# Identity products on TensorE ahead of the first input, a second queue allowed for a load, and a new order of work

## The chip, the cores and the metric

The kernel runs on one core of a Trainium2 chip. The metric is the device time of one execution in microseconds (us). The engines are named as in the profile: PE is TensorE's matrix products, PEld its loads of the stationary operand, DVE is VectorE, ACT is ScalarE, POOL is GpSimd, SP is SyncE, which here only issues DMAs.

## The reference, cut to what matters

Two sequence models run side by side on 2048 steps of 640 channels, and their outputs are put next to each other. The first is a diagonal complex state-space recurrence, the second a gated long convolution.

```python
def _A_ref(x, Lambda_re, Lambda_im, B_re, B_im, C_re, C_im, log_dt, Dskip):
    Lam = Lambda_re + 1j * Lambda_im
    dt = jnp.exp(log_dt)
    Lam_bar = jnp.exp(dt * Lam)
    B_bar = ((Lam_bar - 1.0) / Lam)[:, None] * Bmat
    Bu = jnp.einsum("bld,pd->blp", x + 0j, B_bar)
    for t in range(L):
        h = Lam_bar[None, :] * h + Bu[:, t, :]
    y = 2.0 * jnp.einsum("blp,dp->bld", hseq, Cmat).real + x * Dskip[None, None, :]

def _B_ref(q, k, v, shift_k, ssm_k, ssm_D):
    k_shift = k_shift + k_pad[:, t:t + S, :] * shift_k[:, ks - 1 - t]   # four taps
    kv = k_shift * v
    y = irfft(rfft(kv) * rfft(ssm_k))[:, :S] + kv * ssm_D
    return q * y

return jnp.concatenate([a, b], axis=-1)
```

## The kernel before

**Tiling.** The 640 channels are five blocks of 128, with index j for the states of the first model and G for the channels of the second (there called group). Time in the first model is split into four phases s of 512 steps each (steps 4m + s), so that one scan over 512 steps serves four.

**First model.** `x{s}` loads phase s of x by a DMA that transposes (line 182, on SyncE's queue, 0.66 MB each). `B{j}` loads the real and the imaginary rows of B (line 176, two DMAs each). For j = 0 and 1 TensorE transposes B by products with the identity (`bt{j}`, line 480) and the result is copied to BT (`be{j}`, line 462 on ScalarE, 460 on VectorE); for j = 2, 3, 4 it multiplies B by a diagonal of gamma instead (`bg`, lines 494 to 497), for which VectorE builds the diagonals (`dG`, line 381, tile H). `v{s}_{j}` is the group of products that makes the input of phase s for block j: five products with x for the real part and five for the imaginary part (line 515), and, for all phases but s = 1, two more each with the evicted state of the phase before and a diagonal of Lam_bar (lines 517 and 518, 14 products in all); `ve{s}_{j}` evicts it. The diagonals are `dL` (line 381, tile diagL). So a group with s = 2 needs `ve1` of its block, one with s = 3 needs `ve2`. Phase 0 is turned by a table of sines and cosines (`rs`), scanned (`sc`, line 544) and turned back (`ra`, `rout`); `oa`, `od` (lines 556 to 564) carry the states to the other phases. `p{i}_{s}` projects 128 steps of phase s to the output (20 products of 320 columns, line 577, and six for the skip, line 582), `yo` evicts it (line 599, ScalarE), `yd` stores it.

**Parameters.** A short chain on VectorE and ScalarE makes the numbers of the first model from five small loads `lv0` to `lv4`: `tv` transposes them on TensorE (line 322), `tve` copies them out, then `exp`, `rho`, `rr`, `Fi` (lines 350 to 361), the sine and cosine `trig1` (line 368, 163, 164), `lam` (lines 375 to 378), `dL`, and gamma (`den`, lines 408 to 411, and `gam`, lines 418 to 426, nine small operations, on GpSimd where the table says so). `diagD` and `drhs`, `dcol` (lines 381, 248, 256) are for the skips.

**Second model.** For each of five groups G: k and v come by transposing loads; `kS` is a copy of k with its halves exchanged (line 618 on VectorE, 616 on ScalarE); `tap` is the four-tap filter on TensorE (line 641), `kv` the product with v (line 646). The long convolution is a Fourier transform in two steps on TensorE: `s1h`, `s1k` (line 657) and `s2h`, `s2k` (line 670) for the filter and for kv, each with evictions of 1024 columns to As_h, As_kv, Hf, Xs; then the product of the two spectra on VectorE, in two halves (`ya`, `y`, lines 682 to 688); then four inverse steps (`inv`, lines 696 to 699) evicted to zz (`zs`), two transposing DMAs of zz (`zt`), two final steps on TensorE (`fin`, line 715), the product with q on VectorE (`ob`, line 720) and the store (`od_`). The halves of `y` feed two inverse steps each.

**What sets the order.** No scheduler runs. A plan names 165 or so steps with an engine, a cost and what they need, and a table of text, ORDER, gives the order in which they are issued. Each engine works its own steps strictly in that order, each waiting for what it needs. `@n` after a name is the PSUM buffer that the step uses (four buffers of two banks, 0, 2, 4, 6), `!` sends the step to its other engine. ORDER was found by a search over a model of the engines, outside the kernel.

Of the kernel before, what the change touches and what calls it, by code (L numbers as in the profile page):

```python
# [919 lines left out]


ORDER = """
lv3! pc lsk lv4! lv0 B0 pc2 dc3 dc lv2! zer lv1! pc3 dc2 B1 pk dsel x1 gp0 tsk@0 bt0@2 gp1 tske@0 dS0 tv@4 be0@2 tve@4 bt1@6 pp
x2 drhs dD exp dcm@0 be1@6 rho Fi rr den v1_0@4 tp0 dcol@0 trig1 G0 prr lam tp1 v1_1@2 dL1 x3 pow ve1_0@4 dL0 tab1 dL2 ve1_1!@2
v2_0@6 gam! tab0 kT0 G1 tp3 dG B2 v2_1@0 tp2 x0 tab3 ve2_0!@6 gp3 tab2 v3_0@4 ve2_1!@0 gp2 kS0 B4 aRM tp4 vT0 G3 dRM tap0_0@2
hp0 tap0_1@6 ve3_0!@4 tab4 bg0@0 dS1 v0_0@4 bge0!@0 H0 B3 hp1 CT0 H1 hp2 kv0_0@2 v3_1@0 ve0_0@4 kv0_1@6 hp3 H2 hs0 rs0 bg3@2
kvo0 ve3_1@0 bg1@4 kT1 sc0 H3 bg2@6 v0_1@0 bge2@6 ra0 bge3@2 bge1@4 rout0 v1_2@6 oa2_0 ve0_1@0 od2_0 G2 v1_3@2 rs1 CT1 ve1_2@6
ca0 v2_2@4 sc1 ve1_3@2 kvs0 kS1! had0 oa3_0 vT1 s1h0_3@0 s1h0_1@6 od3_0 v2_3@2 s1he0_1@6 ra1 s1he0_3@0 ve2_2@4 rout1 s1h0_0@6
oa2_1 ve2_3@2 tap1_1@0 od2_1 s1he0_0@6 s1h0_2@4 v3_2@2 s1he0_2@4 oa1_1 cs0 tap1_0@6 qi0 ve3_2@2 od1_1 hs1 s1k0_2@4 ca1 v0_2@2
dS2 kT2 kv1_0@6 s1ke0_2@4 kv1_1@0 s1k0_3@6 cs1 ve0_2@2 s2h0_0@4 s2h0_2@0 s1ke0_3@6 v3_3@2 rs2 s2he0_0@4 kvo1 s2he0_2@0 sc2  # L930
s1k0_1@6 ve3_3@2 s2h0_1@4 s1k0_0@0 s1ke0_1@6 v0_3@2 ra2 s1ke0_0@0 s2he0_1@4 rout2 oa2_2 s2k0_1@6 ve0_3@2 kS2 s2k0_0@0 vT2
s2h0_3@4 s2ke0_1@6 had1 od2_2 v1_4@2 s2ke0_0@0 rs3 s2he0_3@4 kvs1 s2k0_3@6 ve1_4@2 s2k0_2@0 s1h1_0@4 sc3 s2ke0_3@6 v2_4@2
s2ke0_2@0 s1he1_0@4 ya0_0 tap2_0@6 ve2_4@2 s1h1_3@0 kv2_0@6 tap2_1@4 s1he1_3@0 s1k1_3@2 kT3 kv2_1@4 s1k1_0@6 s1ke1_3@2 s1k1_2@0
dS3 s1ke1_0@6 s1h1_1@4 s1h1_2@2 nH s1ke1_2@0 v3_4@6 y0_0 kvo2 hs2 s1he1_1@4 ya0_1 s1he1_2@2 s2h1_0@0 ve3_4@6 s2h1_3@4 y0_1
s1k1_1@2 kS3! v0_4@6 ra3 s1ke1_1@2 rout3 vT3 s2he1_0@0 oa2_3 inv0_2@2 ve0_4@6 od2_3 inv0_1@0 zs0_2@2 tap3_0@6 had2 rs4 s2he1_3@4
s2h1_2@2 kvs2 zs0_1@0 inv0_0@4 sc4 s2he1_2@2 s2h1_1@0 zs0_0@4 inv0_3@2 s2he1_1@0 s2k1_0@4 kv3_0@6 zs0_3@2 s2k1_3@0 ra4 s2k1_2@6
s2ke1_0@4 zt0_0 tap3_1@2 s2ke1_2@6 rout4 s2k1_1@4 oa2_4 s2ke1_3@0 p1_0@6 kT4 kv3_1@2 s2ke1_1@4 od2_4 s1k2_0@0 dS4 kvo3 yo1_0@6
s1k2_1@4 zt0_1 p0_2@2 oa3_2 s1ke2_0@0 od3_2 s1ke2_1@4 oa1_0 p0_0@6 od1_0 yo0_2@2 kS4! ya1_1 yd1_0 yd0_2 s1k2_3@0 yo0_0@6 vT4
s1k2_2@4 s1h2_0@2 y1_1 s1ke2_3@0 p2_0@6 s1ke2_2@4 ya1_0 kvs3 s1he2_0@2 yd0_0 inv1_2@0 yo2_0@6 y1_0 fin0_0@4 yd2_0 zs1_2@0
s1h2_1@2 inv1_3@6 ob0_0@4 s1he2_1@2 fin0_1@0 oa1_3 zs1_3@6 s1h2_2@4 s1h2_3@2 ob0_1@0 s1he2_2@4 inv1_1@6 hs3 s1he2_3@2 od1_3  # L940
inv1_0@4 od_0 zs1_1@6 s2h2_1@0 oa3_4 s2k2_3@2 zs1_0@4 s2k2_1@6 od3_4 s2he2_1@0 zt1_1 p2_2@4 s2ke2_3@2 oa1_2 s2ke2_1@6 od1_2
s2k2_2@0 oa1_4 yo2_2@4 s2k2_0@2 s2ke2_2@0 od1_4 s2h2_0@6 tap4_0@4 s2he2_0@6 oa3_3 s1k3_1@0 s2ke2_0@2 yd2_2 s1k3_3@6 zt1_0
kv4_0@4 s1ke3_1@0 s1k3_0@2 od3_3 s1ke3_0@2 tap4_1@4 s1ke3_3@6 s1k3_2@0 s2h2_3@2 had3 ya2_0 s1ke3_2@0 s1h3_3@6 qi1 s2he2_3@2
s2h2_2@0 s2he2_2@0 kv4_1@4 fin1_1@2 s1he3_3@6 s1h3_1@0 y2_0 kvo4 s1h3_0@4 s1he3_1@0 s1h3_2@6 hs4 ya2_1 s1he3_0@4 inv2_1@0
s1he3_2@6 inv2_0@4 zs2_1@0 s2h3_0@6 y2_1 zs2_0@4 fin1_0@0 ob1_1@2 s2he3_0@6 inv2_3@4 kvs4 ob1_0@0 inv2_2@6 zs2_3@4 s2k3_0@2
zs2_2@6 oa3_1 od_1 s2k3_1@0 s2h3_1@4 s2ke3_0!@2 s2ke3_1@0 zt2_1 s2h3_3@6 s2he3_1@4 s2he3_3!@6 s2k3_3@0 s2k3_2@2 s2ke3_3@0 p0_1@4
od3_1 s2ke3_2@2 had4 ya3_0 s2h3_2@6 yo0_1@4 s1h4_1@0 s2he3_2@6 y3_0 s1h4_0@2 p1_1@4 s1he4_1@0 zt2_0 ya3_1 s1he4_0@2 s1k4_0@6
yo1_1@4 y3_1 s1h4_3@0 s1h4_2@2 s1ke4_0@6 inv3_0@4 yd0_1 s1he4_2!@2 s1he4_3@0 yd1_1 inv3_2@6 qi2 inv3_3@0 zs3_2@6 zs3_0!@4
inv3_1@2 zs3_3@0 fin2_1@6 zs3_1!@2 p0_3@4 zt3_1 s1k4_1@0 ob2_1@6 yo0_3@4 fin2_0@2 yd0_3 s1k4_2@4 s1ke4_1!@0 zt3_0 s1k4_3@6
s1ke4_2@4 ob2_0@2 s1ke4_3@6 s2h4_2@0 s2h4_3@4 s2he4_2!@0 s2k4_3@6 s2he4_3@4 s2k4_1@2 od_2 s2ke4_3@6 s2k4_2@0 p3_2@4 s2ke4_2@0  # L950
s2ke4_1@2 ya4_1 s2k4_0@6 yo3_2@4 s2h4_1@0 y4_1 s2ke4_0@6 yd3_2 s2h4_0@2 p1_2@4 s2he4_1@0 qi3 s2he4_0!@2 ya4_0 inv4_2@6 yo1_2@4
inv4_3@0 y4_0 yd1_2 zs4_2@6 fin3_1@2 zs4_3@0 fin3_0@4 inv4_1@6 ob3_1@2 inv4_0@0 zs4_1@6 ob3_0@4 p3_1@2 zs4_0@0 od_3 zt4_1 p3_3@6
zt4_0 p1_3@4 p2_1@0 qi4 yo1_3@4 yd1_3 p3_0@4 yo2_1@0 yd2_1 yo3_1@2 yd3_1 fin4_0@0 yo3_0@4 fin4_1@2 ob4_0@0 yd3_0 p2_3@4 yo3_3@6
ob4_1@2 yd3_3 od_4 yo2_3@4 yd2_3
"""


# [66 lines left out]
```

## Time and profile before

| | us |
|---|---|
| median of three runs | 204.2 |
| lowest, highest | 203.26, 204.62 |
| profiled execution, its time | 204.2 |
| profiled execution, its span | 202.3 |

| engine | busy us of the span |
|---|---|
| PE | 186.3 |
| DVE | 167.8 |
| ACT | 153.3 |
| POOL | 27.0 |

The profile is one execution, read from its first instruction to its last; 1.9 us of its time lie outside that span. A row of the timeline has the start, the duration, the engine, the source line, the operation, what it writes and reads, how many of them are merged, and in brackets how long the engine was idle before it and what ended that. Products of TensorE are pipelined: a product of 512 columns is given 0.38 us, though the next one starts sooner, so the spacing of starts says more than the duration, and a busy TensorE isn't one at its peak. A row of the grouped view has the count, the total, the mean in ns, and the idle time ahead of the group.

### The profile page before, as it was taken

How to read it: one execution, taken by the hardware profiler on the slowest of the kernel's cores; microseconds unless marked ns; L12 is line 12 of the kernel's file. 1: busy time of each engine (PE TensorE's matmuls, PEld its weight loads, DVE VectorE, ACT ScalarE, POOL GpSimd, SP SyncE). 2: the span in 40 equal slices, each digit the busy share in tenths (PEclk: the TensorE clock that was granted, in tenths of full speed). 3: DMA queues.
4: the chain of work that ended last, by engine and by line, in shares of the span. 5: the costliest groups of instructions: out<-in, count | busy, mean ns of one | idle time of the engine just before them, and what ended most of it. 6: DMA issues, size and time to landing. Idle time of an engine off the chain costs nothing.

```text
span 202.3 us, 7486 instructions
## 1 busy us (share of the span) xinstructions
PE 186.3 (92%) x3330; PEld 128.3 (63%) x3330; DVE 167.8 (83%) x277; ACT 153.3 (76%) x188; POOL 27.0 (13%) x64
## 2 busy tenths in 40 slices
...
GB/s 115 215 220 252 222 212 217 197 185 177 66 145 200 115 3 19 243 132 135 95 249 222 191 91 186 187 200 143 165 177 169 119 192 127 146 84 196 171 133 136
DMA packets 124909, 32.61 MB, mean 161 GB/s; under 512 B 120903, under 2 KB 124236, under 8 KB 124876
## 3 DMA queue, kind: packets, MB, share of 16 engines
...
q8 instruction: 26, 0.43, 0.8%
...
## 4 chain that ended last, share of the span: by engine, by line
PE 33%; DVE 16%; ACT 9%; issue 3%; DVEq 0%
PE ps L577 15%; PE ps L670 5%; ACT Hf L462 2%; PE ps L657 2%; DVE rot L563 2%; DVE vT L646 2%; ACT zz L462 2%; DVE rot L682 2%; DVE hs L564 2%; DVE Xs L683 2%; PE ps L582 2%; PE ps L715 1%; PE ps L696 1%; ACT As_h L462 1%; DVE rot L556 1%
## 5 line engine op out<-in xcount | busy, mean ns | idle before, releaser
L515 PE MATMUL ps<-xT,BT 128*128 128x512 bf16 x200 | 50.6, 393 | 2.1 <-DMA xT<-in_A_x_dram 2.1
L577 PE MATMUL ps<-Cs,hs 128*128 128x320 bf16 x240 | 36.3, 299 | 0.2
L515 PEld LDWEIGHTS <-BT 128*128 128x128 bf16 x200 | 19.3, 101 | 25.8 <-issue 5.9
L599 ACT CAST BT<-ps 128x640 bf16<-128x640 f32 x16 | 11.0, 692 | 27.4 <-PE ps L582 26.6
L577 PEld LDWEIGHTS <-hs 128*128 128x128 bf16 x240 | 22.0, 98 | 8.1
L720 DVE TENSOR_TENSOR qb<-ps,qb 128x1024 bf16<-128x1024 f32 x10 | 11.9, 1219 | 15.7 <-PE ps L715 15.4
L670 PEld LDWEIGHTS <-G 128*64 128x64 bf16 x640 | 19.4, 112 | 5.3 <-issue 4.3
L462 ACT CAST As_kv<-ps 128x1024 bf16<-128x1024 f32 x19 | 18.5, 1027 | 2.1 <-PE ps L657 2.1
L462 ACT CAST zz<-ps 128x1024 bf16<-128x1024 f32 x18 | 18.0, 1040 | 1.7 <-PE ps L699 1.7
L462 ACT CAST Xs<-ps 128x1024 bf16<-128x1024 f32 x19 | 18.6, 1059 | 0.5 <-PE ps L670 0.5
L462 ACT CAST As_h<-ps 128x1024 bf16<-128x1024 f32 x19 | 18.6, 1031 | 0.3 <-PE ps L657 0.3
L696 PE MATMUL ps<-Xs,H 128*128 128x128 bf16 x80 | 17.5, 219 | 1.0 <-ACT As_h L462 0.5
L462 ACT CAST Hf<-ps 128x1024 bf16<-128x1024 f32 x17 | 17.6, 1044 | 0.3 <-PE ps L670 0.3
L699 PE MATMUL ps<-Xs,H 128*128 128x128 bf16 x80 | 17.5, 219 | 0.0
L698 PE MATMUL ps<-Xs,H 128*128 128x128 bf16 x80 | 17.5, 219 | 0.0
L697 PE MATMUL ps<-Xs,H 128*128 128x128 bf16 x80 | 17.5, 219 | 0.0
L682 DVE TENSOR_TENSOR rot<-Xs,Hf 128x2048 bf16<-128x2048 bf16 x10 | 12.3, 1226 | 3.4 <-ACT Xs L462 2.7
L688 DVE TENSOR_TENSOR Xs<-Xs,rot 128x1024 bf16<-128x1024 bf16 x20 | 12.9, 688 | 0.3
L670 PE MATMUL ps<-As_h,G 128*64 128x128 bf16 x320 | 12.7, 227 | 0.3 <-DVE As_kv L460 0.2
L683 DVE TENSOR_TENSOR Xs<-Xs,Hf 128x2048 bf16<-128x2048 bf16 x10 | 12.2, 1225 | 0.5
L670 PE MATMUL ps<-As_kv,G 128*64 128x128 bf16 x320 | 11.2, 220 | 1.1 <-issue 0.4
L641 PE MATMUL ps<-kT,diagS 64*64 64x512 bf16 x80 | 11.0, 391 | 1.2 <-DVE vT L646 1.2
...
## 6 DMA issues: line engine op xcount, KB each, us to landing
...
```

Source lines behind the costliest of these rows:

```text
L462: self.nc.scalar.copy(out=out, in_=in_)
L515: mm(o, lhsT=self.BT[:, r, k, j * 128:(j + 1) * 128], rhs=xT[:, k, :], start=(k == 0), stop=(s == 1 and k == NT - 1))
L577: mm(o[:, 0:320], lhsT=h[:, r, ts], rhs=self.Cs[:, r, j, c0:c0 + 320], start=(j == 0 and r == 0), stop=(not on_pe and j == NT - 1 and r == 1))
L670: self.nc.tensor.matmul(o[64 * e:64 * e + 64, c:c + 128], lhsT=self.G[:, r, k, :], rhs=As[:, k, :], start=True, stop=True)
L682: tt(out=self.cross(), in0=X[:, ::-1, :], in1=self.Hf[:, 1:2, hs].to_broadcast([128, 2, 1024]), op=ALU.mult)
L683: tt(out=X, in0=X, in1=self.Hf[:, 0:1, hs].to_broadcast([128, 2, 1024]), op=ALU.mult)
L688: self.nc.vector.tensor_tensor(out=X[:, r, :], in0=X[:, r, :], in1=cr[:, r, :], op=ALU.add if r else ALU.subtract)
L696: mm(o_re, lhsT=self.H[:, 0, k1, :], rhs=yre, start=True, stop=False)
L697: mm(o_re, lhsT=self.H[:, 2, k1, :], rhs=yim, start=False, stop=True)
L698: mm(o_im, lhsT=self.H[:, 1, k1, :], rhs=yre, start=True, stop=False)
L699: mm(o_im, lhsT=self.H[:, 0, k1, :], rhs=yim, start=False, stop=True)
L720: self.nc.vector.tensor_tensor(out=self.qb[:, :, cs].rearrange("p a (i c) -> p a i c", c=4), in0=ps[:].rearrange("p a n -> p (a n)").rearr ...
```

## The change

There are three edits. The first adds five steps `wm0` to `wm4` on TensorE, each of which multiplies the 128x128 identity with four copies of itself side by side (512 columns) twice, into a PSUM buffer that nobody reads. They need the identity, and in part a step before them; `tsk` and the first groups of input products name them as needs, which bears only on the search, since both are on TensorE. The second lets a load of B be marked for ScalarE's queue. The third is a new ORDER; in it no load of B is marked.

```diff
+    def pe_warm(self, n, ps):
+        w = self.ident[:].rearrange("p (o d) -> p o d", o=1).to_broadcast([128, 4, 128])
+        for i in range(n):
+            self.nc.tensor.matmul(ps[:, i % 2, :], lhsT=self.ident[:], rhs=w, start=True, stop=True)
...
-        dma(f"B{j}", "SP", 0.95, 1.3, (), lambda e, j=j: K.load_B(e, j))
+        dma(f"B{j}", "SP", 0.95, 1.3, (), lambda e, j=j: K.load_B(e, j), alt=("ACT", 0.8))
...
+    WM = []
+    for n, (w, d) in enumerate(((2, "dc"), (2, "wm0"), (2, "bt0"), (2, "bt1"), (2, "wm3"))):
+        A(f"wm{n}", "PE", 0.43 * w, [d], lambda ps, w=w: K.pe_warm(w, ps), take=f"wm{n}", give=f"wm{n}")
+        WM.append(f"wm{n}")
...
-    A("tsk", "PE", 1.0, ["dc", "lsk"], lambda ps: K.pe_sk(ps), take="tsk")
+    A("tsk", "PE", 1.0, ["dc", "lsk", "wm1"], lambda ps: K.pe_sk(ps), take="tsk")
...
-            A(f"v{s}_{j}", "PE", (10 if s == 1 else 14) * P512, XE[s] + BE[j] + ([] if s == 1 else dL + [f"ve{(s - 1) % 4}_{j}"]) + (["zer"] if s == 0 else []),
+            A(f"v{s}_{j}", "PE", (10 if s == 1 else 14) * P512, XE[s] + BE[j] + (WM if s == 1 else dL + [f"ve{(s - 1) % 4}_{j}"]) + (["zer"] if s == 0 else []),
...
-ob4_1@2 yd3_3 od_4 yo2_3@4 yd2_3
...
+p1_1@6 yo1_3@2 yd1_3 p2_1@2 yo1_1@6 qi4 yd1_1 p3_1@6 yo2_1@2 yd2_1 yo2_3@0 yd2_3 fin4_1@2 yo3_1@6 fin4_0@0 ob4_1@2 yd3_1 p3_2@6
+yo3_3@4 ob4_0@0 yd3_3 od_4 yo3_2@6 yd3_2
```

TensorE, just ahead of its first product with x, before the change (numbers after a name are those of the buffer):

```order
L480 LDWEIGHTS As_kv_160
L480 MATMUL ps3_67<-ident_69,As_kv_160 128x128
L253 LDWEIGHTS dsel_119
L253 MATMUL ps0_64<-drhs_121,dsel_119 128x160
L515 LDWEIGHTS BT_130
L515 MATMUL ps2_66<-xT1_136,BT_130 128x512
```

and after it, where line 323 is the identity product and the lines below it stand five or more further down:

```order
L323 LDWEIGHTS ident_69
L323 MATMUL ps1_65<-ident_69 128x512
L323 LDWEIGHTS ident_69
L323 MATMUL ps0_64<-ident_69 128x512
L323 LDWEIGHTS ident_69
L323 MATMUL ps0_64<-ident_69 128x512
L520 LDWEIGHTS BT_130
L520 MATMUL ps1_65<-xT1_136,BT_130 128x512
```

Of the ten identity products four stand first of all on TensorE, two between the transposes of B's two blocks, and four ahead of the products with x. The product for dcol (line 253) has moved behind them, and the first group is that of block 1, no longer of block 0.

VectorE between the end of the parameter chain and the evictions of the first groups, before:

```order
L375 TENSOR_TENSOR lam_99<-rr_87,cos1_93 128x5
L376 TENSOR_TENSOR lam_99<-rr_87,sin1_91 128x5
L377 TENSOR_SCALAR lam_99<-lam_99 128x5
L378 CAST lamb_82<-lam_99 128x15
L381 TENSOR_TENSOR diagL_133<-ident_69,lamb_82 128x640 x3
L460 CAST hs1_142<-ps1_65 128x1024
L381 TENSOR_TENSOR H_128<-ident_69,gamb_83 128x384 x3
L460 CAST hs0_140<-ps3_67 128x1024
L460 CAST hs1_142<-ps0_64 128x1024
L618 COPY kS_154<-kT_153 64x1032 x2
```

and after; first what stands between Fi and lam:

```order
L366 CAST Fi_97<-fr_89 128x5
L465 COPY BT_130<-ps3_67 128x10x128
L386 TENSOR_TENSOR diagD_132<-ident_69,vecb_124 128x640
L248 TENSOR_TENSOR drhs_121<-dmask_120,vecb_124 128x160
L380 TENSOR_TENSOR lam_99<-rr_87,cos1_93 128x5
```

then what follows diagL, from the last three of gamma's nine operations on:

```order
L429 TENSOR_TENSOR gam_98<-pq_84,rden_95 128x10
L430 TENSOR_SCALAR gam_98<-gam_98 128x10
L431 CAST gamb_83<-gam_98 128x15
L465 CAST hs0_140<-ps2_66 128x1024
L256 CAST dcol_b_118<-ps0_64 128x160
L386 TENSOR_TENSOR H_128<-ident_69,gamb_83 128x384 x3
L465 CAST hs1_142<-ps3_67 128x1024
L282 TENSOR_TENSOR R_125<-r_cv_115,r_mask_112 128x128
```

The copy of B's first block (line 465) and gamma (lines 423 to 431) have come to VectorE, the first from ScalarE, the second from GpSimd; diagD and drhs, which stood ahead of Fi, stand behind it. The first of the casts to hs1 (block 1) has gone to ScalarE; the second, on which the group of phase 3 for block 1 waits, stands behind dG (tile H) as one of the casts did before.

VectorE between the product of the spectra of group 3 and that of group 4, before:

```order
L460 CAST As_h_159<-ps1_65 128x2x32x16
L460 CAST zz_162<-ps2_66 128x8x32x4
L460 CAST zz_162<-ps1_65 128x8x32x4
L720 TENSOR_TENSOR qb_158<-ps3_67,qb_158 128x16x64
L460 CAST As_kv_160<-ps0_64 128x2x32x16
L720 TENSOR_TENSOR qb_158<-ps1_65,qb_158 128x16x64
L460 CAST Hf_161<-ps0_64 128x2x512
L682 TENSOR_TENSOR rot_152<-Xs_139,Hf_161 128x2048
L683 TENSOR_TENSOR Xs_139<-Xs_139,Hf_161 128x2048
L688 TENSOR_TENSOR Xs_139<-Xs_139,rot_152 128x1024 x2
L460 CAST Hf_161<-ps1_65 128x2x512
L682 TENSOR_TENSOR rot_152<-Xs_139,Hf_161 128x2048
```

and after:

```order
L561 TENSOR_SCALAR rot_152<-hs0_140,lam_99 128x1024
L562 TENSOR_SCALAR rot_152<-hs0_140,lam_99 128x512
L563 TENSOR_SCALAR rot_152<-hs0_140,lam_99 128x512
L568 TENSOR_TENSOR rot_152<-rot_152,h30_141 128x1024
L569 TENSOR_TENSOR h30_141<-rot_152 128x2x512
L465 CAST zz_162<-ps3_67 128x8x32x4
L465 CAST zz_162<-ps0_64 128x8x32x4
L465 CAST Hf_161<-ps0_64 128x2x512
L725 TENSOR_TENSOR qb_158<-ps3_67,qb_158 128x16x64
L725 TENSOR_TENSOR qb_158<-ps1_65,qb_158 128x16x64
L687 TENSOR_TENSOR rot_152<-Xs_139,Hf_161 128x2048
L688 TENSOR_TENSOR Xs_139<-Xs_139,Hf_161 128x2048
```

Three evictions have gone from there, the carrying of a state (od3_0, block 0 to phase 3) has come. On TensorE, six projections stand behind the last product of group 4 before the change and seven after it.

More of the change, by code (lines that the diff above doesn't have):

```diff
@@ L922 @@
 ORDER = """
[L923 to L952, printed above, removed]
@@ L953 @@
-zt4_0 p1_3@4 p2_1@0 qi4 yo1_3@4 yd1_3 p3_0@4 yo2_1@0 yd2_1 yo3_1@2 yd3_1 fin4_0@0 yo3_0@4 fin4_1@2 ob4_0@0 yd3_0 p2_3@4 yo3_3@6
-ob4_1@2 yd3_3 od_4 yo2_3@4 yd2_3
+lv1! pc lsk lv0! lv4 B0 pc2 dc dc3 wm0@0 lv2! zer lv3! pc3 dc2 wm1@2 B1 gp1 dsel x1 tsk@4 gp0 bt0@6 tske@4 dS0 tv@0 wm2@2 pp
+tve@0 bt1@4 x2 pk den exp wm3@2 be1@4 rho Fi wm4@0 rr be0!@6 v1_1@2 tp0 dD trig1 prr drhs G1 lam tp1 v1_0@4 x3 dL1 pow ve1_1@2
+dL2 dL0 tab0 dcm@0 gam v2_1@6 gp3 aRM vT0 ve1_0!@4 tab1 tp2 dcol@0 dG B3 v2_0@2 G3 kT0 tp3 ve2_1!@6 tab2 dRM v3_1@4 ve2_0!@2
@@ new lines @@
+od2_4 kS4! s1h2_3@4 s1k2_2@6 p1_0@2 oa1_1 od1_1 zt0_1 yo0_0@0 s1ke2_2@6 dS4 s1he2_3@4 ya1_1 s1k2_1@0 s1h2_0@6 yo1_0@2 yd0_0
+p0_2@4 vT4 s1ke2_1@0 s1he2_0@6 y1_1 ya1_0 s1h2_2@2 yd1_0 yo0_2@4 s1k2_0@0 hs3 s1k2_3@6 s1he2_2@2 p1_2@4 s1ke2_0@0 kvs3 y1_0
+s1ke2_3@6 yd0_2 oa1_3 s2h2_1@2 od1_3 yo1_2@4 s2h2_2@0 s2he2_1@2 yd1_2 fin0_1@6 oa1_0 inv1_0@4 s2he2_2@0 od1_0 s2h2_0@2 zs1_0@4
+fin0_0@0 s2he2_0@2 inv1_1@4 ob0_1@6 inv1_2@2 zs1_1@4 oa3_2 inv1_3@6 zs1_2@2 ob0_0@0 s2k2_0@4 zs1_3@6 od3_2 s2k2_1@2 od_0
@@ new lines @@
+s2k2_3@0 s2ke2_0@4 zt1_0 s2k2_2@6 oa1_4 s2ke2_1@2 tap4_1@4 od1_4 s2ke2_2@6 s1k3_3@2 s1ke3_3@2 s2h2_3@6 kv4_1@4 s2ke2_3@0
+s1k3_2@2 ya2_0 s1k3_0@4 s2he2_3@6 zt1_1 p2_2@0 s1ke3_2@2 s1ke3_0@4 had3 y2_0 qi1 s1h3_1@6 ya2_1 yo2_2@0 s1h3_0@2 tap4_0@4
+s1he3_1@6 yd2_2 s1h3_2@0 s1he3_0@2 s1k3_1@6 kv4_0@4 s1ke3_1@6 inv2_0@2 s1he3_2@0 y2_1 fin1_0@6 kvo4 s1h3_3@4 zs2_0@2 inv2_1@0
+hs4 oa3_3 s1he3_3@4 inv2_2@2 od3_3 zs2_1@0 s2h3_3@4 zs2_2@2 oa3_4 s2h3_1@0 s2he3_1@0 ob1_0@6 fin1_1@2 s2he3_3@4 s2k3_0@0 ob1_1@2
```

19 lines of the change are left out of this document (added).

## The prediction

> **What bounds the kernel now.** I read the page first, then busy time by stage with the granted clock, then the timeline of the front and the chain of waits at the end.
>
> ```profile
> span 202.3 us, 7486 instructions
> PE 186.3 (92%) x3330; PEld 128.3 (63%) x3330; DVE 167.8 (83%) x277; ACT 153.3 (76%) x188; POOL 27.0 (13%) x64
> ```
>
> No engine is idle for long, so one average can't say what limits. The next view gives busy time in stretches of 3.41 us; the columns are stretch, length, busy us (instructions) of TensorE, its weight loads, VectorE, ScalarE and GpSimd, granted clock, DMA share and GB/s.
>
> ```profile
> core 0: us, PE busy (x) PEld busy (x) DVE busy (x) ACT busy (x) POOL busy (x), PEclk, DMA share, GB/s
> 0.49:3.90 3.41, 1.27 (x14) 1.10 (x15) 2.52 (x30) 1.28 (x1) 3.08 (x17) 1.00 0.33 99
> 3.90:7.31 3.41, 2.81 (x22) 2.06 (x21) 3.38 (x7) 1.91 (x3) 3.17 (x6) 1.00 0.84 212
> 7.31:10.73 3.42, 1.31 (x4) 0.47 (x4) 3.11 (x14) 3.23 (x8) 2.78 (x9) 1.00 1.08 231
> 10.73:14.14 3.41, 3.41 (x10) 1.17 (x9) 3.31 (x9) 1.53 (x4) 3.07 (x6) 1.00 1.12 215
> ...
> 126.77:130.18 3.41, 1.70 (x109) 1.14 (x97) 3.34 (x7) 3.41 (x5) 0.00 (x0) 1.00 1.24 161
> 130.18:133.59 3.41, 3.41 (x98) 2.78 (x96) 3.38 (x5) 2.17 (x3) 0.00 (x0) 0.50 1.00 227
> ```
>
> Two things are to be seen. TensorE ran at a clock of 0.50 from 130.18 to 133.59, right after a stretch in which it was busy for 1.70 of 3.41 us. And the column says 1.00 at the front, where the spacing of the weight loads says something else:
>
> ```profile
> 9.42 0.10 PEld L515 LDWEIGHTS <-BT 128*128 128x128 bf16 x1 [2.32 <-issue]
> ...
> 13.64 0.15 PEld L515 LDWEIGHTS <-BT 128*128 128x128 bf16 x1 [0.28 <-issue]
> 14.07 2.73 PEld L515 LDWEIGHTS <-BT 128*128 128x128 bf16 x13 [0.28 <-issue]
> ```
> ```profile
> 9.42 7.87 PE L515 MATMUL ps<-xT,BT 128*128 128x512 bf16 x25 [2.14 <-DMA xT<-in_A_x_dram]
> ...
> 23.17 0.38 PE L517 MATMUL ps<-hs,diagL 128*128 128x512 bf16 x1
> ```
>
> From 9.42 to 13.64 there are ten steps of 0.42 us, from 14.07 on thirteen loads in 2.73, 0.21 each. So eleven products ran at half rate, and 11 x 0.21 = 2.3 us were lost there; the clock's column misses what happened before 14.14.
>
> [...]
>
> **The front.**
>
> ```profile
> 2.02 0.31 DVE L211 TENSOR_SCALAR ident<-ident 128x128 bf16<-128x128 bf16 x1
> ```
>
> This makes the identity; the new order has it first on VectorE, one operation of 0.31 from about 1.2, so it is there at 1.5 rather than 2.33. The change puts ten identity products (512 columns, 0.42 us each at half rate, 4.2 us in all) ahead of 9.42. TensorE is busy there for 1.27 + 2.81 = 4.1 us, so 5.3 are idle, 1.5 of them before the identity exists. 4.2 into 3.8 spills by up to 0.4 us, which moves the first real product from 9.42 to 9.8 at worst and leaves no gap ahead of it. At best the clock is free by then, and the 2.3 us are saved: 20 products at 0.21 end at 13.7 rather than at 16.2, two more groups of 14 (3.0 us each) follow, and after five products of its own (1.1) the fifth input group's first product on an evicted state, at 23.17 now, comes at 20.9. [...]
>
> But that product also waits for VectorE, and there the order changes.
>
> ```profile
> 6.63 0.31 DVE L248 TENSOR_TENSOR drhs<-dmask,vecb 128x160 bf16<-128x160 bf16 x1
> 6.86 0.81 DVE L381 TENSOR_TENSOR diagD<-ident,vecb 128x640 bf16<-128x640 bf16 x1
> ...
> 8.57 0.17 DVE L359 TENSOR_SCALAR fr<-fr 128x5 f32<-128x5 f32 x1
> ...
> 8.98 0.17 DVE L361 CAST Fi<-fr 128x5 int32<-128x5 f32 x1
> ...
> 10.88 0.85 DVE L375 TENSOR_TENSOR lam<-rr,cos 128x5 f32<-128x5 f32 x1
> ...
> 12.04 0.23 DVE L378 CAST lamb<-lam 128x15 bf16<-128x15 f32 x1
> 12.31 2.30 DVE L381 TENSOR_TENSOR diagL<-ident,lamb 128x640 bf16<-128x640 bf16 x3
> 16.25 1.23 DVE L460 CAST hs<-ps 128x1024 bf16<-128x1024 f32 x1 [1.64 <-PE ps L515]
> 17.93 3.17 DVE L381 TENSOR_TENSOR H<-ident,gamb 128x384 bf16<-128x384 bf16 x3 [0.46 <-POOL gamb L426]
> 21.02 2.50 DVE L460 CAST hs<-ps 128x1024 bf16<-128x1024 f32 x2
> ```
> ```profile
> 6.73 1.23 ACT L462 COPY BT<-ps 128x1280 bf16<-128x1280 bf16 x1 [0.33 <-PE ps L480]
> ...
> 9.94 0.30 ACT L164 ACTIVATE cos<-aph,hpi 128x5 f32<-128x5 f32 x1
> ```
>
> VectorE now waits 1.64 us for TensorE at 16.25 and 0.46 for GpSimd's gamma at 17.93. In the changed order, after Fi (9.15, taken as unmoved: den's four small operations now go ahead of it, drhs and diagD leave), come: the copy of B's first block, taken over from ScalarE (no row on VectorE: 1.23 is ScalarE's for the same copy; the L460 row scaled to 1280 gives 1.53), diagD 0.81, drhs 0.31, so lam starts at 11.5 rather than 10.88. The other way in, through ScalarE, gives the same: its copy of B's second block comes up to 1.2 us later behind the identity products, and the cosine's end goes from 10.24 to 11.4. Lam takes 1.39 (10.88 to 12.27), diagL 2.30: 15.2. Then gamma's nine small operations, now on VectorE, at 0.20 from one start to the next (8.57 to 8.98 is two): 17.0; a cast of 1.23: 18.2; dcol, like drhs, 0.31: 18.5; dG 3.17: 21.7; the cast that the fifth group waits for: 22.9. That is 0.3 us ahead of 23.17.
>
> The soft term is dG: three products of 384 columns took 1.06 us each, while those of 640 before them took 0.77, so 1.5 in all if nothing slows them, the product is then ready at 21.2, and the front gains 2.0. GpSimd has phase tables to make in that stretch before and after the change, so I stay nearer to the upper price and take a **front gain of 0.7 us**, with 0 and 2.0 as its ends. [...]
>
> B's loads may go by ScalarE's queue, but the new table marks none of them so: nothing moves, 0. The loads of x keep their places on SyncE's queue, x1 behind four small and four B loads as now, so its landing stays at 9.42.
>
> **The middle.** VectorE gets 1.2 (the copy) and 1.8 (gamma) more, both in the front and counted there, and gives one swap of k to ScalarE:
>
> ```profile
> L618 DVE COPY kS<-kT 64x1032 bf16<-64x1032 bf16 x4 | 2.4, 612 | 0.1
> ...
> L616 ACT COPY kS<-kT 64x1032 bf16<-64x1032 bf16 x6 | 6.3, 1050 | 0.1
> ```
>
> That is 1.2 us less for VectorE and 2.1 more for ScalarE, which loses the 1.23 copy. Full evictions of 1024 columns on VectorE are 13 before and after. The steps are the same otherwise, so I carry the lead of the front through at its size, with the 0.50 stretch left in place.
>
> **The end.** From 177 on TensorE has no gap. The first view is VectorE's timeline, the second the chain of waits.
>
> ```profile
> 153.71 1.29 DVE L688 TENSOR_TENSOR Xs<-Xs,rot 128x1024 bf16<-128x1024 bf16 x2
> ...
> 157.90 1.23 DVE L460 CAST zz<-ps 128x1024 bf16<-128x1024 f32 x1 [0.64 <-PE ps L699]
> 159.44 1.23 DVE L720 TENSOR_TENSOR qb<-ps,qb 128x1024 bf16<-128x1024 f32 x1 [0.31 <-DMA qb<-in_B_q_dram]
> 161.84 1.23 DVE L460 CAST As_kv<-ps 128x1024 bf16<-128x1024 f32 x1 [1.17 <-PE ps L657]
> ...
> 168.01 1.23 DVE L682 TENSOR_TENSOR rot<-Xs,Hf 128x2048 bf16<-128x2048 bf16 x1 [2.69 <-ACT Xs L462]
> ...
> 175.58 1.29 DVE L688 TENSOR_TENSOR Xs<-Xs,rot 128x1024 bf16<-128x1024 bf16 x2
> ```
> ```profile
> 176.31 0.93 PE ps L715 x32
> 179.03 1.36 PE ps L577 x10
> ...
> 194.02 0.93 PE ps L715 x32
> 194.96 1.36 PE ps L577 x10
> ...
> 198.00 0.69 ACT BT L599
> ```
>
> After the last product of the spectra (channel group 4, 176.87) TensorE has two inverse steps (177.24 to 179.03, 0.9 each), five projections (179.03 to 194.02, 3.0 each), two final steps (0.93) and a sixth projection: 20.8 us. The new order leaves three inverse steps, one and two final steps and seven projections: 2.7 + 0.5 + 0.9 + 21.0 = 25.1. It breaks even only if that product ends by 198.0 - 25.1 = 172.9, 4.0 us sooner. VectorE has from 155.0 to 176.87 now: eight evictions or outputs (9.8), two groups of products (3.78 each, 168.01 to 171.8), and 4.8 of waiting, the four waits above. In the new order it is the last state's 2.3 (put there in place of evictions), five evictions or outputs (6.1) and the same two groups: 15.9 plus the waiting. With 155.0 - 0.7 + 15.9 = 170.2, there is room for 2.7 us of waiting. Between the two products the new order has two projections where three stand now, 3.0 us less ahead of the work that VectorE waits for, so I expect the waits to shrink by about that, from 4.8 to some 2, and TensorE to stay the bound.
>
> **Sum.** The profiled execution took 204.2 us, 1.9 over its span of 202.3, and is itself the median of the three runs (203.26 to 204.62). 204.2 - 0.7 + 0 + 0 = **203.5 us**.
>
> **The rivals.**
> Forecast, chance 0.34: as summed, 202.0 to 204.3.
> B, the new order also fills TensorE's hole before 130, so that the 0.50 stretch goes: 3.41 x 0.5 = 1.7 us less, 201.8; with the front's ends, 200.5 to 202.5. For it: the hole is a wait in a stretch where VectorE was busy for 3.34 of 3.41 us, and VectorE comes there a little sooner. Against: nothing in the order is aimed at it. 0.30.
> C, slower: the end stage gets its seventh projection and the waits of 4.8 us before the last product stay. Then it ends at 155.0 - 0.7 + 15.9 + 4.8 = 175.0, 2.1 after the break-even of 172.9: 206.3, and 207.0 without the lead of the front. It decides from a product later than 172.9. For it: four separate waits on three engines make up the 4.8. Against: with fewer projections ahead, TensorE should feed VectorE sooner. 0.26.
> D, the identity products don't open the clock and the front gains nothing: 204.2 and 0.3 either way. For it: from 3.90 to 7.31 TensorE was busy for 2.81 of 3.41 us, and still the products at 9.42 ran at half rate. Against: the added products join up with the real ones without a gap. 0.10.
>
> A measurement of this kernel can tell about 1% from no change, that is below 202.16 or above 206.24. Faster by more: seven tenths of B (0.21) and a seventh of the forecast (0.05), 0.26. Slower by more: two thirds of C (0.17) and 0.02 for stalls that no case names, 0.19. Within: 0.55. The range of 201.0 to 206.9 leaves out a fifth of B and a third of C, some 0.15 in all.
>
> **What would show it.** Right: weight loads 0.21 apart from the first real product on; VectorE without its wait of 1.64 at 16; the fifth group's first product on a state at 21 to 23; the last product of the spectra before 172.9; TensorE without a gap from there. Wrong: steps of 0.42 after 9.42 (D); that product after 173 (C); no stretch at 0.50 (B). A stall of TensorE between 35 and 150 that isn't there now would break the sum where it simply carries the lead.

## The result and the profile after

Beside the kernel before on the same chip, the changed kernel took 201.44 us (median of 4 runs, 201.35 to 201.58) against 203.73 (4 runs, 203.24 to 204.62): a ratio of 0.9883, with a 95% interval from 0.9842 to 0.9925. The forecast was 203.5 with a range of 201.0 to 206.9. In the two profiled executions the span went from 202.33 to 199.58. Lines of the changed kernel stand five later from `pe_vec` on (515 is now 520).

First the page of the changed kernel, its span and busy times:

```profile
span 199.6 us, 7503 instructions
PE 186.4 (93%) x3328; PEld 128.3 (64%) x3340; DVE 164.9 (83%) x285; ACT 153.8 (77%) x189; POOL 24.8 (12%) x55
```

TensorE is as busy as before (186.4 against 186.3), although ten products were added and the weight loads of the front stand 0.21 us apart from 10.03 on rather than from 14.07; VectorE has 2.9 us less, where the prediction gave it 1.8 more (1.2 for the copy, 1.8 for gamma, 1.2 off for a swap). That is the first hint at the step that failed.

Busy time by stretches of 3.41 us, in the front and around the place where TensorE had its hole before (columns as in the prediction):

```profile
3.34:6.75 3.41, 3.41 (x29) 2.51 (x29) 2.26 (x9) 0.21 (x1) 3.17 (x6) 1.00 0.76 200
6.75:10.16 3.41, 3.13 (x15) 1.49 (x14) 3.13 (x13) 2.44 (x3) 2.66 (x9) 1.00 1.08 222
...
122.90:126.31 3.41, 2.04 (x103) 1.70 (x91) 3.38 (x5) 3.41 (x5) 0.00 (x0) 1.00 1.08 165
126.31:129.72 3.41, 3.41 (x93) 2.61 (x94) 3.27 (x6) 2.38 (x4) 0.00 (x0) 1.00 1.20 165
```

The record of the granted clock begins at 10.16 here, and at 14.14 before; further down this is called the opening of the clock. The hole is still there (2.04 of 3.41), but shallower than 1.70, and the stretch behind it ran at 1.00 rather than 0.50.

The timeline of the front, weight loads first, then the fifth input group's first product on an evicted state:

```profile
9.65 0.10 PEld L520 LDWEIGHTS <-BT 128*128 128x128 bf16 x1 [0.57 <-issue]
10.03 3.83 PEld L520 LDWEIGHTS <-BT 128*128 128x128 bf16 x18 [0.27 <-issue]
```
```profile
15.34 0.38 PE L522 MATMUL ps<-hs,diagL 128*128 128x512 bf16 x1
18.36 0.38 PE L522 MATMUL ps<-hs,diagL 128*128 128x512 bf16 x1
21.91 0.38 PE L522 MATMUL ps<-hs,diagL 128*128 128x512 bf16 x1 [0.35 <-DVE hs L465]
```

From the second real product on the loads stand 0.21 apart. From its first product on a state to that of the next group, the third input group takes 3.02 us (15.34 to 18.36) and the fourth 3.55 (to 21.91): there TensorE waits for an eviction on VectorE, so VectorE is the gate at the fifth group, as the prediction said. Its own timeline:

```profile
8.78 0.82 DVE L465 COPY BT<-ps 128x1280 bf16<-128x1280 bf16 x1
9.51 1.16 DVE L386 TENSOR_TENSOR diagD<-ident,vecb 128x640 bf16<-128x640 bf16 x1
...
14.76 0.16 DVE L423 TENSOR_SCALAR nn<-lam 128x5 f32<-128x5 f32 x1
...
16.12 1.21 DVE L465 CAST hs<-ps 128x1024 bf16<-128x1024 f32 x1
...
17.49 3.23 DVE L386 TENSOR_TENSOR H<-ident,gamb 128x384 bf16<-128x384 bf16 x3
20.64 1.21 DVE L465 CAST hs<-ps 128x1024 bf16<-128x1024 f32 x1
```

The order of the steps is the predicted one; they end at 21.85 instead of 22.9.

The end, VectorE's timeline and then the chain of waits:

```profile
157.63 1.22 DVE L465 CAST Hf<-ps 128x1024 bf16<-128x1024 f32 x1 [0.84 <-PE ps L675]
...
160.40 1.22 DVE L725 TENSOR_TENSOR qb<-ps,qb 128x1024 bf16<-128x1024 f32 x1 [0.41 <-PE ps L720]
...
165.79 1.23 DVE L687 TENSOR_TENSOR rot<-Xs,Hf 128x2048 bf16<-128x2048 bf16 x1 [0.46 <-ACT BT L604]
...
168.31 1.29 DVE L693 TENSOR_TENSOR Xs<-Xs,rot 128x1024 bf16<-128x1024 bf16 x2
```
```profile
172.91 1.36 PE ps L582 x10
...
190.90 0.93 PE ps L720 x32
191.83 1.37 PE ps L582 x10
...
194.87 0.69 ACT BT L604
```

The last product of the spectra ends at 169.60, 3.3 us ahead of the break-even of 172.9; three waits of together 1.7 us stand where four of 4.8 stood, and behind it the chain is TensorE alone.

Where the 2.75 us of the span come from is seen in three stretches, cut on VectorE at the end of the fourth group's products of the spectra and of the fifth's: first before, then after.

```profile
0.00:155.00 155.00, 144.25 (x2664) 94.24 (x2665) 146.31 (x258) 133.10 (x165) 26.99 (x64) 0.99 0.86 166
155.00:176.88 21.88, 20.94 (x444) 17.75 (x441) 16.83 (x18) 13.71 (x16) 0.00 (x0) 1.00 0.72 151
176.88:202.33 25.45, 21.08 (x233) 16.34 (x229) 4.65 (x4) 6.53 (x9) 0.00 (x0) 0.99 0.64 143
```
```profile
0.00:152.19 152.19, 144.44 (x2726) 94.20 (x2739) 143.51 (x263) 133.44 (x165) 24.79 (x55) 1.00 0.86 167
152.19:169.60 17.41, 16.75 (x336) 14.39 (x326) 15.53 (x18) 13.06 (x16) 0.00 (x0) 1.00 0.75 155
169.60:199.58 29.98, 25.18 (x277) 19.67 (x276) 5.84 (x6) 7.27 (x10) 0.00 (x0) 0.97 0.66 148
```

The second stretch is 4.47 shorter and the third 4.53 longer: the end comes to nothing, as forecast. The whole gain is there at the first cut, 2.81 us. Up to that cut VectorE is idle for 155.00 - 146.31 = 8.69 before and 152.19 - 143.51 = 8.68 after, and busy for 2.80 less. So the lead equals work that VectorE no longer has ahead of it, taken over the whole of that stretch; its two halves differ, as shown further down.

### The profile page after: what moved, and what is told of

Same layout as the page of the kernel before. It is cut to its first block, busy times and chain, and to the rows that moved or that the text cites. A ratio compares the mean times of both kernels' runs of the same rounds, so it can differ in the third digit from the quotient of the medians.

```text
span 199.6 us, 7503 instructions
## 1 busy us (share of the span) xinstructions
PE 186.4 (93%) x3328; PEld 128.3 (64%) x3340; DVE 164.9 (83%) x285; ACT 153.8 (77%) x189; POOL 24.8 (12%) x55
## 5 line engine op out<-in xcount | busy, mean ns | idle before, releaser
L520 PE MATMUL ps<-xT,BT 128*128 128x512 bf16 x188 | 47.8, 381 | 0.9 <-DMA xT<-in_A_x_dram 0.3
L520 PEld LDWEIGHTS <-BT 128*128 128x128 bf16 x200 | 18.7, 98 | 22.6 <-issue 1.3
L725 DVE TENSOR_TENSOR qb<-ps,qb 128x1024 bf16<-128x1024 f32 x10 | 11.9, 1216 | 15.9 <-PE ps L720 15.9
L467 ACT CAST As_kv<-ps 128x1024 bf16<-128x1024 f32 x20 | 20.0, 1041 | 0.3 <-PE ps L662 0.3
L467 ACT CAST As_h<-ps 128x1024 bf16<-128x1024 f32 x20 | 19.8, 1040 | 0.0
L467 ACT CAST Hf<-ps 128x1024 bf16<-128x1024 f32 x19 | 19.3, 1042 | 0.0
L467 ACT CAST zz<-ps 128x1024 bf16<-128x1024 f32 x17 | 17.2, 1034 | 2.1 <-PE ps L704 2.1
L675 PE MATMUL ps<-As_kv,G 128*64 128x128 bf16 x320 | 11.7, 221 | 1.0 <-DVE vT L651 0.5
L675 PE MATMUL ps<-As_h,G 128*64 128x128 bf16 x320 | 11.7, 221 | 0.7 <-ACT Xs L467 0.7
L651 DVE TENSOR_TENSOR vT<-ps,vT 128x1024 bf16<-128x1024 f32 x10 | 11.9, 1213 | 0.4 <-PE ps L646 0.4
```

Of the source, the lines that this page charges most:

```text
L467: self.nc.scalar.copy(out=out, in_=in_)
L520: mm(o, lhsT=self.BT[:, r, k, j * 128:(j + 1) * 128], rhs=xT[:, k, :], start=(k == 0), stop=(s == 1 and k == NT - 1))
L651: self.nc.vector.tensor_tensor(out=self.vT[:, ts], in0=ps[:].rearrange("p a n -> p (a n)"), in1=self.vT[:, ts], op=ALU.mult)
L675: self.nc.tensor.matmul(o[64 * e:64 * e + 64, c:c + 128], lhsT=self.G[:, r, k, :], rhs=As[:, k, :], start=True, stop=True)
```

## The experiments

Each run stood beside the kernel before on its own chip; that one's medians were 204.04 (first four runs), 203.88 (the four with spare work or the moved load) and 204.0 (the last four). The edits of the order are shown by the few names around them.

**The changed kernel once more.** Nothing is edited.

> The changed kernel once more, as the mark for the other three on the same chip. All theories: 201.4 us within 0.4, a ratio to the kernel before of 0.985 to 0.992, and no stretch at half clock between the front and the end.

201.73 us (6 runs, 201.52 to 202.19), ratio 0.9895 [0.9864, 0.9926]. In this execution the clock opened at 8.02 rather than 10.16, the first product on a state came at 14.93 rather than 15.34, and the fifth group at 21.91 in both. What TensorE gains beyond that is lost at the gate again.

**The new order without the identity products.**

```diff
-dc3 wm0@0 lv2!
+dc3 lv2!
...
-dc2 wm1@2 B1
+dc2 B1
...
-tv@0 wm2@2 pp
+tv@0 pp
...
-exp wm3@2 be1@4 rho Fi wm4@0 rr
+exp be1@4 rho Fi rr
```

> The new order without its ten identity products. Theory 1 (the front's lead is held back by VectorE, and the other half of the gain is the half-clock stretch at 130 that is gone): the clock opens 3.4 to 5 us after the first real product instead of 0.5, the fifth input group's state product comes at 22.5 to 23.2 instead of 21.9, and the end is 0.6 to 1.3 us later than the changed kernel, some 202.4. Theory 2 (the identity products are the whole gain): 203.7, as before the change. Theory 3 (the order is the whole gain, the front is gated by VectorE anyway): 201.4 to 201.7.

202.83 us (12 runs, 201.89 to 203.84), ratio 0.994 [0.9916, 0.9964]. The order by itself is worth 1.2 us, the identity products in it 1.1. Timeline of TensorE, then its stretch up to the same cut:

```profile
23.49 0.38 PE L522 MATMUL ps<-hs,diagL 128*128 128x512 bf16 x1
```
```profile
0.00:153.76 153.76, 141.72 (x2716) 93.28 (x2729) 143.96 (x263) 133.48 (x165) 24.01 (x55) 1.00 0.85 166
```

The fifth group doesn't wait here: TensorE itself comes at 23.49. At the cut this kernel leads the one before by 1.24, with 2.35 less work on VectorE and 9.80 of idle time rather than 8.69. Both parts of the gain are thus seen on VectorE: the order takes work from it, the identity products take 1.1 of waiting.

**The identity products in the old order.**

```diff
-gp0 tsk@0 bt0@2
+gp0 wm0@0 wm1@2 tsk@0 bt0@2
...
-tve@4 bt1@6
+tve@4 wm2@0 bt1@6
...
-den v1_0@4
+den wm3@2 wm4@2 v1_0@4
```

> The old order with the ten identity products put in at the same places of the front. Theory 1: the front of TensorE leads by up to 1.2 us (its fifth input group waits for a cast behind VectorE's diagonals), the half-clock stretch near 130 comes or stays away by chance, 202.3 to 203.2. Theory 2: 201.4. Theory 3: 203.4 to 203.8.

205.09 us (12 runs, 203.07 to 205.76), ratio 1.0036 [1.0008, 1.0064]: slower by 1.05. The clock opened at 11.32 rather than 14.14, and it helped nothing, as two rows of TensorE say:

```profile
6.46 0.20 PE L327 MATMUL ps<-ident,As_h 25*128 25x25 bf16 x1
...
23.09 0.38 PE L522 MATMUL ps<-hs,diagL 128*128 128x512 bf16 x1 [0.67 <-DVE hs L465]
```

In this order VectorE's gate stands at 23.1, where TensorE came by itself at 23.17. The timeline of before has the parameters' transpose sooner:

```profile
4.97 0.20 PE L322 MATMUL ps<-ident,As_h 25*128 25x25 bf16 x1
```

With the identity products it stands behind four of them and comes at 6.46, and Fi ends at 10.03 instead of 9.15. So the same ten products are worth -1.1 in one order and +1.05 in the other.

**TensorE's hole filled in the old order.** Four identity products are put where TensorE waits ahead of 130; the front is the old one.

```diff
+    A("wf", "PE", 0.43, ["dc"], lambda ps: K.pe_warm(4, ps), take="wf", give="wf")
...
-s1ke3_0@2 tap4_1@4
+s1ke3_0@2 wf@0 tap4_1@4
```

> The old order without identity products in the front, but with four identity products in TensorE's wait at 128 to 129.5, which nobody reads. Theory 1: no half-clock stretch at 130, so 1.0 to 1.7 us less than the kernel before wherever that has one: 202.2 to 202.9. Rival (the stretch at half clock lies beside VectorE's chain and costs nothing): 203.5 to 204. Where the added products collide with the work behind them: up to 0.9 us slower.

204.56 us (12 runs, 202.91 to 206.21), ratio 1.0015 [0.9986, 1.0044]. The half-clock stretch is gone (mean granted clock 0.997 rather than 0.990), and no time with it; a gain of 1.7 would have been 0.9917. VectorE's timeline, the last group's products:

```profile
168.27 1.23 DVE L687 TENSOR_TENSOR rot<-Xs,Hf 128x2048 bf16<-128x2048 bf16 x1 [2.74 <-ACT Xs L467]
...
175.84 1.29 DVE L693 TENSOR_TENSOR Xs<-Xs,rot 128x1024 bf16<-128x1024 bf16 x2
```

VectorE ends the fourth group's products at 154.56 rather than 155.00, then waits 2.74 us for ScalarE, and ends its last product at 177.14, against 176.88. But the run can't price the stretch, since most executions of the kernel before don't have it. One stretch of 3.41 us at half clock takes 0.8% off the mean granted clock of 202 us. Of the 69 runs of the kernel before beside these experiments, the two slowest left out, 15 had a mean clock of 0.986 to 0.991 and a median of 204.70 us, and 52 had 0.995 or more and a median of 203.85. So executions that, by their mean clock, have the stretch took 0.85 us longer, whether through the stretch itself or through the wait ahead of it (1.70 of 3.41 us busy). This run, with all of its mean clocks at 0.997 or more, stands 0.6 to 0.7 above the executions without the stretch, so the four products themselves cost something here.

**Spare work on VectorE, at three places.** Two of the operations that build the diagonals of lambda are done again with the same values (1.55 us), in the changed kernel: ahead of the fifth group's products, behind them, or in the middle.

```diff
+    A("vf", "DVE", 1.6, ["lam"], lambda: [K.dve_diagL(q) for q in (0, 1)])
...
-ya4_1 p0_3@2
+vf ya4_1 p0_3@2
```

> Changed kernel with 1.5 us of spare work on VectorE (two of the operations that build the diagonals of lambda are done a second time, with the same values) just ahead of the last group's products of the spectra. Theory A (from the first group's spectra on VectorE has no slack until that last product, and behind it stand 25.1 us of TensorE work without a gap, so that product sets the end): the last product goes from 169.6 to 171.1 and the end from 201.6 to 203.1. Theory B (TensorE's own work sets the end and VectorE is ahead by more than 1.5 us): the end stays at 201.6.

202.89 us (10 runs, 202.32 to 203.89), ratio 0.9955 [0.9926, 0.9983].

```profile
162.00 1.55 DVE L386 TENSOR_TENSOR diagL<-ident,lamb 128x640 bf16<-128x640 bf16 x2
...
169.89 1.29 DVE L693 TENSOR_TENSOR Xs<-Xs,rot 128x1024 bf16<-128x1024 bf16 x2
```

The last product moved from 169.60 to 171.19, by all of the 1.55, and the median by 1.2 to 1.5 over the changed kernel's two. Without added work ahead of it that product came at 169.60, 169.75 and, in the next run, 170.18, so its move is 1.0 to 1.6 us.

```diff
-y4_0 fin3_0@6
+y4_0 vf fin3_0@6
```

> The same 1.5 us of spare work on VectorE, right behind the last group's products of the spectra. Theory A and theory B both: 201.6, no change, since TensorE has projections enough queued and VectorE only outputs that can wait. Something above 202.5 would say that the outputs behind the products are on the path as well, and then the run with the work ahead of them does not tell A from B.

201.77 us (4 runs, 201.37 to 201.96), ratio 0.9885 [0.9843, 0.9927]: nothing that can be told from the changed kernel's 201.44 and 201.73. The two together say that VectorE sets the end up to its last product and not behind it.

```diff
-had1 ra2 kS2!
+had1 vf ra2 kS2!
```

> The same 1.5 us of spare work on VectorE in the middle, around 62 us, ahead of the third input group's back substitution. Theory A, in its wide form (VectorE without slack all the way from the front to the last product): the last product comes at 171.1 and the time is 203.1. Theory A in its narrow form (VectorE has slack ahead of the first group's spectra at 88 us, where it idles for 6.1 us in all before that point): less than 0.5 us of it arrives, 201.6 to 202.1. Theory B: 201.6.

205.46 us (10 runs, 203.81 to 206.65), ratio 1.0064 [1.0031, 1.0096]. The theory in its wide form expected 203.1; it has the sign and less than half of the size. Stretches, and then a row of TensorE:

```profile
78.13:81.54 3.41, 0.14 (x5) 0.13 (x6) 3.38 (x6) 1.01 (x2) 0.00 (x0) 1.00 0.74 154
81.54:84.96 3.42, 3.42 (x84) 2.12 (x82) 3.32 (x4) 2.49 (x3) 0.00 (x0) 0.50 0.48 152
```
```profile
81.41 0.97 PE L675 MATMUL ps<-As_kv,G 128*64 128x128 bf16 x16 [3.39 <-DVE vT L651]
```

The late VectorE leaves TensorE idle for 3.39 us; the clock then falls to 0.50 for a stretch, the first projection comes 4.4 us later than in the changed kernel, and 4.1 of that arrive at the end of the span. There was no slack in the middle. Part of the excess comes with the clock: two of the ten executions kept it at 1.000 and took 203.81 and 204.29 us; the other eight, with means of 0.980 to 0.992, took 205.04 to 206.65.

**B's second block loaded from ScalarE's queue.**

```diff
-B1 gp1
+B1! gp1
```

> Changed kernel with the load of B's second block issued from ScalarE's queue, which the change allows and the new order does not use. If the front is bound by the landing of x, whose first load is issued right behind that block on SyncE's queue: x lands up to 1 us sooner, the first real product is at 8.6 to 9.2 instead of 9.5, and the time is 200.8 to 201.3. If VectorE is the gate of the front (gamma, the cast, the diagonals of gamma): the first product moves and the fifth group's state product stays at 21.9, 201.6. If the issue on ScalarE delays the exponential: Fi from 8.87 to 9.5, and 202.2.

202.09 us (6 runs, 201.30 to 202.62), ratio 0.9904 [0.987, 0.9937].

```profile
9.28 4.67 PE L520 MATMUL ps<-xT,BT 128*128 128x512 bf16 x20
...
21.93 0.38 PE L522 MATMUL ps<-hs,diagL 128*128 128x512 bf16 x1 [0.79 <-DVE hs L465]
```

The first product came 0.2 to 0.4 sooner than in the two executions of the changed kernel, and the wait at the gate took it; the time is no better than the changed kernel's.

**Part of the identity products.** The last four alone (`wm3`, `wm4`), and the first six alone (`wm0` to `wm2`), in the new order.

```diff
-dc3 wm0@0 lv2!
+dc3 lv2!
...
-dc2 wm1@2 B1
+dc2 B1
...
-tv@0 wm2@2 pp
+tv@0 pp
```
```diff
-exp wm3@2 be1@4 rho Fi wm4@0 rr
+exp be1@4 rho Fi rr
```

> New order with the last four of the ten identity products alone (those behind the transposes of B's blocks). If what opens the clock is dense 512-column work joined to the real products: it opens 1.5 to 3.4 us sooner than without any (13.99), by 12.5, and the time is 201.9 to 202.4, half of the 1.1 us between 202.8 (none) and 201.7 (all). If all ten are needed: 202.8. If these four do all of it: 201.7.

> New order with the first six identity products alone. If only work that joins the real products without a gap counts: the clock opens at 13.5 to 14, as without any, and the time is 202.8. If the sum of work in the stretch before 9.5 counts: it opens by 10.2 and the time is 201.7.

The last four: 200.99 us (8 runs, 200.85 to 202.48), ratio 0.984 [0.9798, 0.9882]. The first six: 201.94 us (6 runs, 201.59 to 203.40), ratio 0.9899 [0.9856, 0.9942]. Both come nearest to the case in which the part alone does what all ten do (201.7), and the four look better than ten, which no case had. For each of the two the profiled execution was the slowest of its runs (202.48 and 203.40), with the clock opening at 13.46 and 15.40, so their medians have no profile. In that of the four, gamma's first operation on VectorE started at 14.29 rather than 14.76, since four products less stand ahead of the parameters' transpose (4.96 rather than 5.43); that would put the gate 0.47 sooner, about what the median gained. The intervals overlap with the changed kernel's, so that it beats it isn't shown.

**Gamma back on GpSimd.**

```diff
-dcm@0 gam v2_1@6
+dcm@0 gam! v2_1@6
```

> Changed kernel with gamma's nine small operations back on GpSimd. If VectorE is the gate of the front: the 1.8 us that VectorE saves are lost again by waiting, since GpSimd's gamma was ready at 17.9 before the change and dG takes over 3 us behind it; the fifth input group's first product on a state comes at 22.0 to 23.2 rather than 21.9, and the time is 201.6 to 202.8. If GpSimd's own work is what slows the diagonals of gamma (3.23 us for three): gamma is later and the diagonals run beside GpSimd's tables as before, no gain either. Faster than 201.2 would say that VectorE's small operations were the dearer place.

201.66 us (6 runs, 201.36 to 202.06), ratio 0.9872 [0.9834, 0.991]: no change, with the fifth group's product at 21.70. Where gamma's nine operations run is worth nothing; the diagonals behind them wait 1.96 us for GpSimd's gamma instead, and then take 2.34 rather than 3.23.

**The identity products in the old order, with B's first copy moved to VectorE.** This was to mend the slower run.

```diff
-tv@4 be0@2 tve@4 bt1@6
+tv@4 tve@4 wm2@0 bt1@6
...
-be1@6 rho Fi rr den v1_0@4
+wm3@4 be1@6 rho Fi wm4@4 rr be0!@2 den v1_0@4
```

> Old order with the ten identity products as in the slower run (205.1), and the copy of B's first block moved from ScalarE to VectorE behind Fi. If that copy ahead of the exponential on ScalarE, late behind the identity products, is what cost it (Fi 10.03 rather than 9.15): Fi is back at 9.0 to 9.3 and the time is 203.4 to 204.0, at or a little below before. If something else in the front cost it: 205. If the front's lead of 0.5 to 1.3 us reaches the end in the old order as well: 202.8.

205.18 us (12 runs, 203.45 to 205.77), ratio 1.0051 [1.0023, 1.008]: my reason fell.

```profile
9.87 0.17 DVE L366 CAST Fi<-fr 128x5 int32<-128x5 f32 x1
```

Fi ends at 10.04, as without the move. What is left, as a guess, is that the identity is made at 2.0 in the old order and at 1.1 in the new one, so the four products ahead of the parameters' transpose start a microsecond later. Two rows of the changed kernel, VectorE and TensorE:

```profile
1.09 0.20 DVE L211 TENSOR_SCALAR ident<-ident 128x128 bf16<-128x128 bf16 x1 [1.09 <-POOL ident L187]
...
5.43 0.20 PE L327 MATMUL ps<-ident,As_h 25*128 25x25 bf16 x1
```

The transpose comes at 5.43 there and at 6.46 in the old order. To make the identity earlier in the old order wasn't tried by itself. Nor is the front all of it: in the first run of the products in the old order VectorE ends the third group's products 0.35 later than before (140.02 to 139.67) and the fifth's 1.44 later.

**One line through all of them.** In each profiled execution stands the end of VectorE's last product of the spectra, and the end of TensorE's last product (a row's rounded start and duration can add up to 0.01 less):

| kernel | spectra | TensorE | between |
|---|---|---|---|
| before | 176.88 | 197.96 | 21.08 |
| old order, identity | 178.32 | 199.40 | 21.08 |
| old order, hole filled | 177.14 | 198.22 | 21.08 |
| old order, identity, copy moved | 177.71 | 198.79 | 21.08 |
| after | 169.60 | 194.84 | 25.24 |
| without identity | 171.46 | 196.69 | 25.23 |
| spare work ahead | 171.19 | 196.42 | 25.23 |
| spare work in the middle | 173.76 | 199.00 | 25.24 |
| first six | 171.55 | 196.78 | 25.23 |
| gamma on GpSimd | 170.04 | 195.28 | 25.24 |

The other four stand at 25.23 to 25.24 as well. Behind that product TensorE runs without a gap, so its time alone sets the end. The prediction's break-even (20.8 and 25.1 us of work) was this line.

## Why the prediction came out as it did

The time fell into the range, 2.1 us under the number and below the summed case's own 202.0 to 204.3. That the range held is owed to the room it left for rival B, whose reason, as shown below, was not what brought the gain.

**Half rate in the front: right.** With the identity products the clock opens at 10.16, against 14.14 before and 13.99 in the new order without them, and rival D is out. Opening it earlier was worth 202.83 - 201.73 = 1.1 us, 0.5%, in the new order.

**The front's gain: mechanism right, size off.** Priced at 0.7, it was 23.17 - 21.91 = 1.26, and 1.36 at the first projection (99.59 to 98.23). VectorE is the gate, shown by six executions in which the clock opened anywhere from 8.02 to 10.53 with the fifth group at 21.91 to 21.93. The 1.05 us by which the chain ended ahead of the predicted 22.9 are the copy at 0.82 rather than 1.23, Fi 0.28 sooner, less 0.35 for a longer diagD, and the first cast, which starts beside gamma's last operation (16.12, when 17.0 was taken). The price of dG, where I stayed near the upper end, was right: 3.23. That GpSimd's tables set this price was my estimate and no run shows it; with gamma back on GpSimd the three took 2.34.

**The middle: this is the step that failed.** "The steps are the same otherwise, so I carry the lead of the front through at its size" gave 0 beyond the front. At the cut the lead is 2.81, 1.45 more than at the first projection, and the kernel without the identity products shows the same 1.45 (from -0.21 to 1.24), so it doesn't come from them. It lies between the first projection and the cut, where VectorE was busy for (stretch, length, busy us, granted clock, DMA share, GB/s), before and then after:

```profile
99.59:155.00 55.41, 53.59 (x82) 0.97 0.96 180
```
```profile
98.23:152.19 53.96, 52.85 (x84) 1.00 0.94 175
```

Of the 1.45, 0.74 is work and 0.71 waiting. Ahead of the first projection it is otherwise: 2.06 of the 2.80 us of work are gone there, but VectorE waits 0.70 longer, so the lead is only 1.36. Which moved steps make the 1.45 isn't separated. Some of it may be the half-clock stretch, which lies in it before (0.97) and not after: in the profile with the hole filled, which has no such stretch, the same way (99.66 to 154.56) took 54.90 rather than 55.41.

In the sum of VectorE's load two things were missing. The last state's 2.3 us was counted into the end and never taken off the stretch ahead of it, which got one eviction (1.2) in exchange. And the change in VectorE's load was summed from the copy, gamma and a swap, while operations that nothing in the diff touches got shorter, as the grouped views show, first of before and then of after:

```profile
L629 DVE TENSOR_TENSOR diagS<-id,sk_b 128x512 bf16<-128x512 bf16 x5 | 4.1, 828 | 0.0
...
L409 DVE TENSOR_TENSOR den<-pq 128x5 f32<-128x5 f32 x1 | 1.0, 1039 | 0.0
L282 DVE TENSOR_TENSOR R<-r_cv,r_mask 128x128 bf16<-128x128 bf16 x1 | 1.0, 1016 | 0.0
```
```profile
L634 DVE TENSOR_TENSOR diagS<-id,sk_b 128x512 bf16<-128x512 bf16 x5 | 3.4, 686 | 0.0
...
L623 DVE COPY kS<-kT 64x1032 bf16<-64x1032 bf16 x2 | 0.9, 435 | 0.1
...
L414 DVE TENSOR_TENSOR den<-pq 128x5 f32<-128x5 f32 x1 | 0.3, 282 | 0.0
L282 DVE TENSOR_TENSOR R<-r_cv,r_mask 128x128 bf16<-128x128 bf16 x1 | 0.3, 274 | 0.0
```

These three give 0.7 + 0.7 + 0.7 = 2.1, and the swap of k 1.5 (2.4 to 0.9) where 1.2 was taken; all of them stand ahead of the first projection. With the last state's work, and against gamma, the copy and the eviction, that makes about 2 of the 2.80; the rest is spread over small rows. All three stand at other places in the order now, beside other work of GpSimd. The run with gamma back on GpSimd has R at the same place of VectorE's order as the changed kernel, and there it takes 0.99 rather than 0.27, from 21.57 to 22.56, beside a product of GpSimd from 21.38 to 22.42. It begins 0.19 us behind GpSimd's product and ends 0.14 behind its end. Likewise `den` before ran from 9.26 to 10.30 beside a product of GpSimd from 9.23 to 10.27; after, beside one of 0.29, it took 0.28. That one of the two engines waits for the other is my reading of these ends; no run shows it by itself. That a microsecond of VectorE's work ahead of the last product is a microsecond at the end is shown by the spare work (1.55 us more there, and TensorE's last product at 196.42 rather than 194.84).

**The end: right at nothing.** Its waits shrank to 1.7, where "some 2" stood, and 17.4 us between the two products, where 15.9 + 2 stood. Had they stayed (C), the shorter way up to the cut would still have left 152.2 + 15.9 + 4.8 = 172.9, just the break-even. C needed the late cut as well.

**B: its number, not its reason.** It gave 201.8 and saw the half-clock stretch go; both came. But 52 of the 67 runs of the kernel before had, by their mean clock, no such stretch and took 203.85 in the median, so its going can't be what separates that from the changed kernel's 201.44 and 201.73. The profiled execution before is one that has it (mean clock 0.990); of the 2.75 between the two spans up to some 0.85 may be the stretch. In the kernel before 0.85 came with it, not 1.7.

**Not settled:** which moved steps make the 1.45 in the middle, and how much of it is the half-clock stretch, why the old order loses 1.05 with the products rather than nothing, and whether the last four alone beat all ten.
